# A new order for the first batch of a float32 attention-and-ELU kernel: states and x loaded first on two queues, a weight product in halves, weight sums moved

## The chip, the core and the metric

One core of one Trainium2 chip. The metric is the device time of one execution in microseconds (us). The median of the fast executions counts; ratios are computed as the mean time of one kernel's fast runs over that of the other's in the same rounds, so they are not quite the ratio of the medians quoted. PE is TensorE, PEld its weight loads, DVE VectorE, ACT ScalarE, POOL GpSimd, SP the engine that issues most transfers.

## The reference, cut to what matters

```python
# x: (8, 8, 512, 64), state: (8, 8, 32, 64); w_in: (512, 2048), w_out: (2048, 512); inputs are float64 or float32
scores = scale * x @ state.T          # softmax over the 32 states
xread  = softmax(scores) @ state      # one row per token
scores2 = scale * state @ x.T         # softmax over the 512 tokens
sread  = softmax(scores2) @ x         # one row per state
rows = concat(xread, sread)           # 8 batches of 544 rows of 512
h = rows @ w_in
g = where(h > 0, h, exp(min(h, 0)) - 1)
out = g @ w_out
```

The weights arrive as float64, and the kernel turns each block of 512 columns into float32 itself, with three instructions on ACT (`convert_1`) and four on DVE (`convert_2`).

## The kernel before

For a batch, the kernel multiplies the states of the batch into w_in once ("M", by groups of 512 columns), so that the first product is `attention weights @ M` (F:0 to F:15) and x @ w_in is never formed. ACT takes exp of each block (R), DVE forms the ELU (E, the "max part"), and PE multiplies by w_out. In batch 0 the second product (O:0 to O:15) follows block by block, because w_out is still arriving; from batch 1 on it is a Strassen-like scheme that needs sums of w_out (`weight_sum`).

Batch 0 runs by a written plan. Each word is one step, and each engine keeps the order of its own steps:

```python
plan = """
    w:0.1 w:0.2 kT kTc x:0.0 xc:0.0 w:1.1 x:0.1 xc:0.1 w:1.2 w:2.1 sc:0 mx:0.0 w:3.1 w:2.2
    w:4.1 mx:0.1 tr:0.0 tr:0.1 ae:0.0 tm:0.0 ae:0.1 w:3.2 ps:0.0 w:5.1 tm:0.1 te:0.0 M:0.0
    ...
    tt:1.1 sr:1 O:15 src:1 M:1.0
""".split()
# w:k.1 / w:k.2  conversion of block k on ACT / on DVE
# kT, kTc        transposes of the states on PE, copy on DVE
# x:b.i, xc:b.i  transposes of x on PE, copies on ACT;  sc:b  scores on PE
# mx tr tm su sd tt attention on DVE;  ps pm on POOL;  ae te on ACT
# sT, sTc        transposes of a on PE, copy on ACT;  sr, src  state read on PE, kept by ACT
# M:b.c, Mc:b.c  M for a group of 512 columns on PE, copies;  F R E O  the two products
```

The loads, the sums and the order switch:

```python
def load_states():
    ...
    sync.dma_start(out=raw[m * NS : (m + 1) * NS, :, c], in_=s_v[m, c])   # 8 of them

load_x(0, [scalar])
fetch()                      # one weight block
raw_states = load_states()
for k in range(NRAW - 2):
    fetch()
...
first_batch()
load_x(2, [sync])
for e in (vector, scalar, gpsimd):
    e.on = False             # from here the build's scheduler may reorder these engines
for i in (1, 2, 4, 3):
    weight_sum(i)
for b in range(1, B):
    batch(b)
```

Of the kernel before, what the change touches and what calls it, by code (L numbers as in the profile page):

```python
# [10 lines left out]
FP32 = mybir.dt.float32  # L11
I32 = mybir.dt.int32
U32 = mybir.dt.uint32
# [12 lines left out]
def kernel(  # L26
# [16 lines left out]
    NS = state.shape[2]  # L43
# [37 lines left out]
    def banks(shape, name):  # L81
        return ps_a.tile(shape, FP32, tag="a", name=name)
# [23 lines left out]
        return ap[:, :, None].to_broadcast(list(ap.shape) + [n])  # L106

    ident = cpool.tile([P, P], FP32, name="ident")
    w_in = cpool.tile([P, NP, DF], FP32, name="w_in")
    w_out = cpool.tile([P, FO, DM], FP32, name="w_out")  # L110

    g_all = cpool.tile([P, FO, S], FP32, name="g_all")
# [15 lines left out]
    def load_states():  # L128
        raw = work.tile([P, B, G, D], FP32, tag="w", name="s_sb")
        s_v = state.rearrange("b (m c) n d -> m c n b d", c=G)  # L130
        for m in range(NP):
            for c in range(G):
                sync.dma_start(out=raw[m * NS : (m + 1) * NS, :, c], in_=s_v[m, c])
        return raw

    def turn_states(raw):
# [2 lines left out]
            transpose(ps[:, b], raw[:, b].rearrange("p c d -> p (c d)"))  # L139

    def load_weights(src):
        k = src.shape[-1]
        raw = work.tile([P, 512], moe_w_in.dtype, tag="w", name="raw")
        sync.dma_start(out=raw.rearrange("p (j k) -> p j k", k=k), in_=src)
        return raw

    def low_words(raw):
        return raw.bitcast(U32).rearrange("p (j w) -> p j w", w=2)[:, :, 0]

    def high_words(raw):  # L150
        return raw.bitcast(U32).rearrange("p (j w) -> p j w", w=2)[:, :, 1]

    def convert_1(dst, raw):

# [27 lines left out]
        )  # L182
        vector.tensor_tensor(out=bits, in0=bits, in1=lo, op=ALU.add)

    def load_w_in(c, n):
        cols = slice(c * 512, (c + 1) * 512)
        raw = load_weights(w_in_v[:, n : n + 1, cols])
        return w_in[:, n, cols], raw

    def load_w_out(fo):  # L190
        raw = load_weights(w_out_v[:, fo : fo + 1])
        return w_out[:, fo], raw

    def turn_x(b, i):

# [15 lines left out]
    def by_state(b, name, rhs):  # L211


        ps = banks([P, G, 512], name)
        for m in range(NP):
            for g in range(G):
                d = slice(g * D, (g + 1) * D)
                matmul(
                    ps[m * NS : (m + 1) * NS, g],
                    kT[d, b, m * NS : (m + 1) * NS],  # L220
                    rhs[m][d],
                    start=True,
                    stop=True,
                    tile_position=(g * D, m * NS),
                )
        return ps

    def scores(b):

        st[b, "s_ps"] = by_state(b, "s_ps", [st[b, m] for m in range(NP)])  # L230



# [98 lines left out]
                in_=ps[:, k : k + B // 2].rearrange("p b m s -> p m b s"),  # L332
            )

    def make_m(b, c):

        cols = slice(c * 512, (c + 1) * 512)
        st[b, "m", c] = by_state(b, "m_ps", [w_in[:, m, cols] for m in range(NP)])

    def copy_m(b, c, engines):  # L340
        m_t[b, c] = mpool.tile([P, G, 512], FP32, name="m_sb")
        for g in range(G):
            engines[g](out=m_t[b, c][:, g], in_=st[b, "m", c][:, g])

    def full_m(b, c):
        make_m(b, c)
# [31 lines left out]
    def ffn1_state(fo):  # L378

        ps = ps_h.tile([P, B * NS], FP32, tag="h", name="h_ps")  # L380
        for co in range(NP):
            matmul(
                ps,
                w_in[:, co, fo * P : (fo + 1) * P],
                st["xT"][:, co].rearrange("p b s -> p (b s)"),
                start=(co == 0),
                stop=(co == NP - 1),
            )
        elu(ps, fo)
# [145 lines left out]
    def first_batch():  # L535





        plan = """
            w:0.1 w:0.2 kT kTc x:0.0 xc:0.0 w:1.1 x:0.1 xc:0.1 w:1.2 w:2.1 sc:0 mx:0.0 w:3.1 w:2.2
            w:4.1 mx:0.1 tr:0.0 tr:0.1 ae:0.0 tm:0.0 ae:0.1 w:3.2 ps:0.0 w:5.1 tm:0.1 te:0.0 M:0.0
            w:6.1 w:4.2 ps:0.1 te:0.1 su:0.0 Mc:0.0 su:0.1 pm:0.0 w:8.1 w:6.2 pm:0.1 w:9.1 tt:0.0
            w:7.1 tt:0.1 w:8.2 F:0 w:10.1 F:1 w:7.2 R:0 w:11.1 E:0 w:5.2 F:2 R:1 O:0 R:2 E:1 w:9.2
            w:12.1 E:2 M:0.1 w:10.2 O:1 w:13.1 w:12.2 Mc:0.1 w:14.1 w:13.2 F:3 w:15.1 O:2 w:11.2 R:3
            w:16.1 E:3 w:15.2 F:4 w:17.1 w:16.2 O:3 R:4 w:18.1 E:4 w:14.2 w:19.1 F:5 sd:0.0 w:20.1
            O:4 w:19.2 R:5 w:20.2 w:21.1 F:6 w:22.1 E:5 M:0.2 w:17.2 R:6 F:7 Mc:0.2 w:22.2 w:23.1
            O:5 E:6 w:24.1 w:18.2 R:7 F:8 w:24.2 O:6 R:8 E:7 w:25.1 E:8 w:21.2 w:26.1 F:9 w:25.2 O:7
            w:27.1 w:23.2 R:9 E:9 F:10 sd:0.1 w:27.2 O:8 R:10 E:10 w:28.1 w:26.2 F:11 w:29.1 w:28.2  # L550
            O:9 R:11 w:29.2 w:30.1 w:31.1 M:0.3 E:11 w:30.2 O:10 Mc:0.3 w:31.2 sT:0 F:12 sTc:0 sr:0
            R:12 E:12 O:11 src:0 x:1.0 F:13 xc:1.0 x:1.1 R:13 F:14 xc:1.1 E:13 sc:1 R:14 O:12 mx:1.0
            E:14 mx:1.1 tr:1.0 tr:1.1 ae:1.0 F:15 tm:1.0 ae:1.1 tm:1.1 ps:1.0 sd:1.0 O:13 R:15
            ps:1.1 sd:1.1 te:1.0 E:15 te:1.1 su:1.0 su:1.1 pm:1.0 sT:1 O:14 sTc:1 pm:1.1 tt:1.0
            tt:1.1 sr:1 O:15 src:1 M:1.0
        """.split()
        make_identity(nc, ident)
        o_ps = [o_bank() for c in range(3)]
        o_ps += [ps_h.tile([P, DM], FP32, tag="h", name="o_ps")]
        order = [lambda n=n: load_w_in(0, n) for n in range(NP)]  # L560
        for c in range(1, FC + 1):
            if c < FC:
                order += [lambda c=c, n=n: load_w_in(c, n) for n in range(NP)]
            order += [lambda fo=fo: load_w_out(fo) for fo in range(4 * c - 4, 4 * c)]
        w, h, e = [], {}, {}

        def fetch():
            if len(w) == 28:
                load_x(1, [sync])
            if len(w) < len(order):  # L570
                w.append(order[len(w)]())

        load_x(0, [scalar])
        fetch()
        raw_states = load_states()
        for k in range(NRAW - 2):
            fetch()
        groups = {
            "mx": column_max, "tr": turn_scores, "ae": column_exp, "tm": row_max,
            "ps": row_subtract, "te": row_exp, "su": row_sum, "pm": row_scale,  # L580
            "tt": turn_tokens, "sd": column_total,
        }
        whole = {
            "sc": scores, "sT": turn_state, "sTc": copy_state, "sr": state_read,
            "src": keep_read,
        }
        for step in plan:
            name, _, num = step.partition(":")
            num = [int(i) for i in num.split(".") if i]
            if name == "kT":  # L590
                turn_states(raw_states)
            elif name == "kTc":
                vector.tensor_copy(out=kT, in_=st["k_ps"])
                fetch()
            elif name in groups:
                groups[name](*num)
            elif name in whole:
                whole[name](*num)
            elif name == "w":
                (convert_1, convert_2)[num[1] - 1](*w[num[0]])  # L600
                if num[1] == 2:
                    fetch()
            elif name == "F":
                h[num[0]] = ffn1(0, num[0])
            elif name == "R":
                e[num[0]] = exp_part(h[num[0]])
            elif name == "E":
                max_part(num[0], e[num[0]], h[num[0]])
            elif name == "O":
                ffn2_row(o_ps, num[0])  # L610
            elif name == "x":
                turn_x(*num)
            elif name == "M":
                make_m(*num)
            elif name == "xc":
                copy_x(*num)
            else:
                assert name == "Mc", step
                copy_m(*num, (scalar.copy, scalar.copy))
        copy_m(1, 0, (scalar.copy, vector.tensor_copy))  # L620
        for i in range(2):
            o_sb = opool.tile([P, 2, DM], FP32, name="o_sb")
            for c in range(2):
                (scalar.copy, vector.tensor_copy)[c](out=o_sb[:, c], in_=o_ps[2 * i + c])
            store(0, i, o_sb)

    def batch(b):
        for fo in range(FO):
            elu(ffn1(b, fo), fo)
            if fo % 4 == 1 and fo // 4 + 1 < FC:  # L630
                full_m(b, fo // 4 + 1)
        nxt = b + 1 < B
        hooks = attention(b + 1) if nxt else []
        if b + 2 < B:
# [28 lines left out]
    load_x(2, [sync])  # L663
    for e in (vector, scalar, gpsimd):
        e.on = False
    for i in (1, 2, 4, 3):
        weight_sum(i)
    for b in range(1, B):
        batch(b)
    states()  # L670
# [30 lines left out]
```

## Time and profile before

| | before |
|---|---|
| median of the runs | 797.74 us (797.61 to 797.83) |
| span of the profiled run | 795.6 us |
| PE / DVE / ACT busy | 95% / 43% / 40% |
| F:0, first product of batch 0, starts | 43.27 us |
| O:0, second product of batch 0, starts | 51.44 us |
| batch 1's first product, second half of its first block | 143.32 us |

The shares of the whole span hide the point: DVE and ACT are near full in the first 110 us and half idle afterwards, and PE is the reverse. The stretch up to O:0 and the seam between batch 0 and batch 1 are the two places where PE is not full.

### The profile page before, as it was taken

Reading aid. Unit: us, or ns where it says so; the run is one execution under the profiler, and the core shown is the slowest. Engines: PE = TensorE matmul, PEld = TensorE weight load, DVE = VectorE, ACT = ScalarE, POOL = GpSimd, SP = SyncE. Lnnn points to the kernel's source line nnn. Section 1 sums busy time; section 2 is a strip of 40 time slices with the busy share of each in tenths; the row PEclk is TensorE's granted clock in tenths of the full one; section 3 lists DMA queues with packets and bytes.
Section 4 is the critical chain, followed back from the end, with each engine's and each line's share of the span. In section 5 each row is a group of like instructions: output and inputs, shape, how many; then the busy total and the mean of one; then the engine's idle time right before and its main releaser. Section 6 shows DMA issues by size and latency. Waiting matters only on the chain.

```text
span 795.6 us, 9330 instructions
## 1 busy us (share of the span) xinstructions
PE 756.3 (95%) x3808; PEld 500.9 (63%) x3808; DVE 343.4 (43%) x577; ACT 320.7 (40%) x596; POOL 34.1 (4%) x38
## 2 busy tenths in 40 slices
PE   2389999999999999999999999999999999999996
PEld 1034454358863887368845885488647884588885
DVE  1899958546024721464135612472146313511140
ACT  2889853562136311642055213631264206400420
POOL 0100002002000010002000200010000200000000
PEclk9979999999999999999999999999999999999999
DMA  9757200400300030001100030003000000000001
GB/s 220 276 158 222 103 1 1 106 1 1 80 27 0 2 80 27 1 0 45 37 26 1 1 80 27 0 1 80 27 0 1 29 0 27 1 26 1 28 0 27
DMA packets 42795, 35.21 MB, mean 44 GB/s; under 512 B 36352, under 2 KB 36352, under 8 KB 42752
## 3 DMA queue, kind: packets, MB, share of 16 engines
q1 hardware_dynamic: 38592, 33.56, 14.6%
q10 hardware_dynamic: 4160, 1.05, 0.7%
q8 instruction: 30, 0.49, 0.3%
q14 instruction: 13, 0.11, 0.0%
HBM read 25.69 MB, written 8.91 MB: 43 GB/s over the span
## 4 chain that ended last, share of the span: by engine, by line
PE 93%; DVE 4%; DMA 1%; ACT 0%; issue 0%; ACTq 0%
PE o_ps L92 52%; PE h_ps L92 32%; PE m_ps L92 4%; PE xT_ps L92 2%; DVE w_in L92 1%; PE s_ps L92 1%; DMA x_sb<-in_x_dram 1%; DVE t_w L92 1%; PE sr_ps L92 1%; PE sT_ps L92 1%; DVE total_t L92 1%; DMA s_sb<-in_state_dram 0%; DVE w_out L92 0%; ACT xT L92 0%; PE k_ps L92 0%; DVE aT L92 0%
## 5 line engine op out<-in xcount | busy, mean ns | idle before, releaser
L92 PE MATMUL o_ps<-w_out,g_all 128*128 128x256 f32 (+1 forms) x1088 | 274.8, 406 | 0.0
L92 PEld LDWEIGHTS o_ps<-w_out,g_all 128*128 128x128 f32 x1088 | 204.2, 190 | 62.8 <-issue 35.8
L92 PE MATMUL h_ps<-aT,m_sb 128*128 128x512 f32 x512 | 232.1, 603 | 9.4 <-DVE aT L92 7.9
L92 PEld LDWEIGHTS h_ps<-aT,m_sb 128*128 128x128 f32 x512 | 96.1, 192 | 139.5 <-issue 112.2
L92 DVE SCALAR_TENSOR_TENSOR g_all<-e_sb,h_ps 128x512 f32<-128x512 f32 (+1 forms) x144 | 94.5, 657 | 193.8 <-ACT e_sb L92 193.8
L92 ACT ACTIVATE e_sb<-h_ps 128x512 f32<-128x512 f32 (+1 forms) x144 | 82.4, 572 | 96.3 <-PE h_ps L92 96.2
L92 ACT COPY o_sb<-o_ps 128x256 f32<-128x256 f32 (+1 forms) x62 | 23.3, 378 | 240.2 <-PE o_ps L92 240.2
L92 PE MATMUL o_ps<-t_w,s 128*128 128x256 f32 x480 | 109.1, 380 | 0.0
L92 PEld LDWEIGHTS o_ps<-t_w,s 128*128 128x128 f32 x480 | 90.2, 190 | 16.8 <-ACT o_sb L92 5.0
L92 ACT ACTIVATE e_sb<-e_sb 128x512 f32<-128x512 f32 (+1 forms) x144 | 87.2, 606 | 4.5
L92 DVE TENSOR_TENSOR o_sb<-o_sb,o_ps 128x256 f32<-128x256 f32 x45 | 18.6, 414 | 158.1 <-issue 82.8
L92 PE MATMUL o_ps<-t_w,g_all 128*128 128x256 f32 x240 | 54.2, 379 | 0.0
L92 PEld LDWEIGHTS o_ps<-t_w,g_all 128*128 128x128 f32 x240 | 45.6, 190 | 6.2
L92 PE MATMUL m_ps<-w_in,kT 64*32 64x512 f32 x512 | 37.6, 615 | 6.9 <-ACT a_s L92 6.9
L92 ACT ACTIVATE raw<-raw 128x512 f32<-128x512 uint32 x64 | 43.6, 681 | 1.0
L92 POOL TENSOR_TENSOR t_sb<-t_sb,top_t 128x512 f32<-128x512 f32 x16 | 16.9, 1061 | 573.0 <-DVE top_t L92 560.3
L92 DVE COPY m_sb<-m_ps 128x512 f32<-128x512 f32 x28 | 19.2, 685 | 42.0 <-ACT m_sb L92 42.0
L92 ACT COPY xT<-xT_ps 128x512 f32<-128x512 f32 x32 | 17.2, 589 | 35.0 <-PE xT_ps L92 35.0
L92 PE MATMUL h_ps<-xT_state,w_in 128*128 128x256 f32 x128 | 27.8, 379 | 0.0
L92 PEld LDWEIGHTS h_ps<-xT_state,w_in 128*128 128x128 f32 x128 | 24.3, 190 | 3.3
L92 PEld LDWEIGHTS m_ps<-w_in,kT 64*32 64x32 f32 x512 | 6.0, 105 | 31.3 <-issue 20.9
L92 ACT COPY m_sb<-m_ps 128x512 f32<-128x512 f32 x36 | 20.3, 576 | 8.5 <-PE m_ps L92 8.5
(54 smaller groups left out, 388.2 us busy)
## 6 DMA issues: line engine op xcount, KB each, us to landing
raw<-in_moe_w_in_dram SPq DMA_DIRECT2D x16, 512.0 KB, 5.0
raw<-in_moe_w_out_dram SPq DMA_DIRECT2D x16, 512.0 KB, 4.9
out_dram<-o_sb SPq DMA_DIRECT2D x16, 512.0 KB, 2.7
x_sb<-in_x_dram SPq DMA_DIRECT2D x28, 256.0 KB, 4.9
x_sb<-in_x_dram ACTq DMA_DIRECT2D x4, 256.0 KB, 6.9
s_sb<-in_state_dram SPq DMA_DIRECT2D x8, 64.0 KB, 5.1
out_dram<-o_sb SPq DMA_DIRECT2D x8, 64.0 KB, 1.7
```

What stands on the lines that cost most here:

```text
L92: ins = getattr(self.engine, name)(*args, **kw)
```

## The change

The intent was to let PE start sooner. States and x are loaded before any weight, half on each of two queues. w_in is loaded and stored by half groups of 256 columns with all four row blocks (two of them per load), so that M's first half needs two converted blocks instead of four. The plan has a new order on all engines. The sums of w_out are written inside batch 1's first product.

```diff
-    w_in = cpool.tile([P, NP, DF], FP32, name="w_in")
+    w_in = cpool.tile([P, 2 * FC, NP, 256], FP32, name="w_in")
...
-                sync.dma_start(out=raw[m * NS : (m + 1) * NS, :, c], in_=s_v[m, c])
+                (sync, scalar)[c].dma_start(out=raw[m * NS : (m + 1) * NS, :, c], in_=s_v[m, c])
...
+    def load_w_in(c, k):
+        h, n = divmod(k, 2)
+        rows = slice(2 * n, 2 * n + 2)
+        cols = slice(c * 512 + h * 256, c * 512 + (h + 1) * 256)
+        return w_in[:, 2 * c + h, rows], load_weights(w_in_v[:, rows, cols])
...
-            w:0.1 w:0.2 kT kTc x:0.0 xc:0.0 w:1.1 x:0.1 xc:0.1 w:1.2 w:2.1 sc:0 mx:0.0 w:3.1 w:2.2
+            kT kTc x:0.0 xc:0.0 w:0.1 x:0.1 xc:0.1 w:0.2 w:1.1 sc:0 mx:0.1 w:2.1 tr:0.1 tr:0.0
+            tm:0.1 w:3.1 tm:0.0 ps:0.1 mx:0.0 w:1.2 ps:0.0 ae:0.1 ae:0.0 te:0.1 sT:0 sd:0.0 sd:0.1
+            te:0.0 su:0.1 sTc:0 su:0.0 pm:0.1 w:4.1 M:0.0.0 w:3.2 pm:0.0 Mc:0.0.0 w:7.1 sr:0 tt:0.1
... (the rest of the plan is new as well)
-        load_x(0, [scalar])
-        fetch()
         raw_states = load_states()
-        for k in range(NRAW - 2):
+        load_x(0, [sync, scalar])
+        for k in range(NRAW - 1):
             fetch()
...
             if fo % 4 == 1 and fo // 4 + 1 < FC:
                 full_m(b, fo // 4 + 1)
+            if b == 1 and fo % 4 == 3:
+                weight_sum((1, 2, 4, 3)[fo // 4])
...
-    for i in (1, 2, 4, 3):
-        weight_sum(i)
```

More of the change, by code (lines that the diff above doesn't have):

```diff
@@ L141, in load_weights @@
     def load_weights(src):
-        k = src.shape[-1]
-        raw = work.tile([P, 512], moe_w_in.dtype, tag="w", name="raw")
-        sync.dma_start(out=raw.rearrange("p (j k) -> p j k", k=k), in_=src)
+        _, n, k = src.shape
+        raw = work.tile([P, n, k], moe_w_in.dtype, tag="w", name="raw")
+        sync.dma_start(out=raw, in_=src)
         return raw
     def low_words(raw):
-        return raw.bitcast(U32).rearrange("p (j w) -> p j w", w=2)[:, :, 0]
+        return raw.bitcast(U32).rearrange("p n (j w) -> p n j w", w=2)[:, :, :, 0]
     def high_words(raw):
-        return raw.bitcast(U32).rearrange("p (j w) -> p j w", w=2)[:, :, 1]
+        return raw.bitcast(U32).rearrange("p n (j w) -> p n j w", w=2)[:, :, :, 1]
     def convert_1(dst, raw):
@@ L183, in convert_2 @@
         vector.tensor_tensor(out=bits, in0=bits, in1=lo, op=ALU.add)
-    def load_w_in(c, n):
-        cols = slice(c * 512, (c + 1) * 512)
-        raw = load_weights(w_in_v[:, n : n + 1, cols])
-        return w_in[:, n, cols], raw
+    def load_w_in(c, k):
[3 more added lines that the diff above has]
+        return w_in[:, 2 * c + h, rows], load_weights(w_in_v[:, rows, cols])
     def load_w_out(fo):
         raw = load_weights(w_out_v[:, fo : fo + 1])
-        return w_out[:, fo], raw
+        return w_out[:, fo : fo + 1], raw
     def turn_x(b, i):
@@ L214, in by_state @@
         ps = banks([P, G, 512], name)
+        _, j, n = rhs[0].shape
         for m in range(NP):
@@ L218, in by_state @@
                 matmul(
-                    ps[m * NS : (m + 1) * NS, g],
+                    ps[m * NS : (m + 1) * NS, g, : j * n].rearrange("p (j n) -> p j n", j=j),
                     kT[d, b, m * NS : (m + 1) * NS],
@@ L228, in scores @@
     def scores(b):
-        st[b, "s_ps"] = by_state(b, "s_ps", [st[b, m] for m in range(NP)])
+        st[b, "s_ps"] = by_state(b, "s_ps", [st[b, m][:, None] for m in range(NP)])
     def column_max(b, g):
@@ L333, in turn_read, with make_m @@
             )
-    def make_m(b, c):
-        cols = slice(c * 512, (c + 1) * 512)
-        st[b, "m", c] = by_state(b, "m_ps", [w_in[:, m, cols] for m in range(NP)])
+    def make_m(b, c, h=None):
+        halves = slice(2 * c, 2 * c + 2) if h is None else slice(2 * c + h, 2 * c + h + 1)
+        st[b, "m", c] = by_state(b, "m_ps", [w_in[:, halves, m] for m in range(NP)])
     def copy_m(b, c, engines):
@@ L343, in copy_m, with copy_half @@
             engines[g](out=m_t[b, c][:, g], in_=st[b, "m", c][:, g])
+    def copy_half(b, c, h):
+        if h == 0:
+            m_t[b, c] = mpool.tile([P, G, 512], FP32, name="m_sb")
+        scalar.copy(
+            out=m_t[b, c][:, :, h * 256 : (h + 1) * 256], in_=st[b, "m", c][:, :, :256]
+        )
     def full_m(b, c):
@@ L383, in ffn1_state @@
                 ps,
-                w_in[:, co, fo * P : (fo + 1) * P],
+                w_in[:, fo // 2, co, fo % 2 * P : (fo % 2 + 1) * P],
                 st["xT"][:, co].rearrange("p b s -> p (b s)"),
@@ L541, in first_batch @@
         plan = """
-            w:0.1 w:0.2 kT kTc x:0.0 xc:0.0 w:1.1 x:0.1 xc:0.1 w:1.2 w:2.1 sc:0 mx:0.0 w:3.1 w:2.2
-            w:4.1 mx:0.1 tr:0.0 tr:0.1 ae:0.0 tm:0.0 ae:0.1 w:3.2 ps:0.0 w:5.1 tm:0.1 te:0.0 M:0.0
-            w:6.1 w:4.2 ps:0.1 te:0.1 su:0.0 Mc:0.0 su:0.1 pm:0.0 w:8.1 w:6.2 pm:0.1 w:9.1 tt:0.0
-            w:7.1 tt:0.1 w:8.2 F:0 w:10.1 F:1 w:7.2 R:0 w:11.1 E:0 w:5.2 F:2 R:1 O:0 R:2 E:1 w:9.2
-            w:12.1 E:2 M:0.1 w:10.2 O:1 w:13.1 w:12.2 Mc:0.1 w:14.1 w:13.2 F:3 w:15.1 O:2 w:11.2 R:3
@@ L547, in first_batch @@
-            w:16.1 E:3 w:15.2 F:4 w:17.1 w:16.2 O:3 R:4 w:18.1 E:4 w:14.2 w:19.1 F:5 sd:0.0 w:20.1
-            O:4 w:19.2 R:5 w:20.2 w:21.1 F:6 w:22.1 E:5 M:0.2 w:17.2 R:6 F:7 Mc:0.2 w:22.2 w:23.1
-            O:5 E:6 w:24.1 w:18.2 R:7 F:8 w:24.2 O:6 R:8 E:7 w:25.1 E:8 w:21.2 w:26.1 F:9 w:25.2 O:7
-            w:27.1 w:23.2 R:9 E:9 F:10 sd:0.1 w:27.2 O:8 R:10 E:10 w:28.1 w:26.2 F:11 w:29.1 w:28.2
-            O:9 R:11 w:29.2 w:30.1 w:31.1 M:0.3 E:11 w:30.2 O:10 Mc:0.3 w:31.2 sT:0 F:12 sTc:0 sr:0
@@ L552, in first_batch @@
-            R:12 E:12 O:11 src:0 x:1.0 F:13 xc:1.0 x:1.1 R:13 F:14 xc:1.1 E:13 sc:1 R:14 O:12 mx:1.0
-            E:14 mx:1.1 tr:1.0 tr:1.1 ae:1.0 F:15 tm:1.0 ae:1.1 tm:1.1 ps:1.0 sd:1.0 O:13 R:15
-            ps:1.1 sd:1.1 te:1.0 E:15 te:1.1 su:1.0 su:1.1 pm:1.0 sT:1 O:14 sTc:1 pm:1.1 tt:1.0
-            tt:1.1 sr:1 O:15 src:1 M:1.0
+            kT kTc x:0.0 xc:0.0 w:0.1 x:0.1 xc:0.1 w:0.2 w:1.1 sc:0 mx:0.1 w:2.1 tr:0.1 tr:0.0
+            tm:0.1 w:3.1 tm:0.0 ps:0.1 mx:0.0 w:1.2 ps:0.0 ae:0.1 ae:0.0 te:0.1 sT:0 sd:0.0 sd:0.1
@@ new lines, in first_batch @@
+            te:0.0 su:0.1 sTc:0 su:0.0 pm:0.1 w:4.1 M:0.0.0 w:3.2 pm:0.0 Mc:0.0.0 w:7.1 sr:0 tt:0.1
+            tt:0.0 w:4.2 F:0 src:0 w:8.1 w:2.2 F:1 R:0 w:5.1 E:0 M:0.0.1 w:8.2 Mc:0.0.1 R:1 F:2
+            w:5.2 w:9.1 O:0 E:1 w:10.1 w:9.2 R:2 F:3 w:10.2 w:6.1 M:0.1.0 O:1 E:2 Mc:0.1.0 w:6.2 R:3
+            w:12.1 E:3 F:4 w:7.2 w:11.1 O:2 w:12.2 w:13.1 R:4 w:11.2 M:0.1.1 F:5 w:14.1 w:13.2 O:3
+            R:5 Mc:0.1.1 E:4 w:16.1 E:5 w:14.2 F:6 w:17.1 M:0.2.0 w:16.2 F:7 R:6 w:15.1 E:6 O:4
+            w:17.2 Mc:0.2.0 w:18.1 w:15.2 F:8 R:7 w:18.2 O:5 w:21.1 E:7 R:8 w:21.2 M:0.2.1 w:19.1
@@ new lines, in first_batch @@
+            O:6 E:8 w:23.1 w:19.2 Mc:0.2.1 F:9 w:23.2 w:24.1 O:7 w:25.1 w:24.2 w:20.1 w:25.2 F:10
+            R:9 O:8 w:20.2 w:22.1 E:9 R:10 w:22.2 M:0.3.0 w:26.1 F:11 E:10 O:9 Mc:0.3.0 w:26.2 R:11
+            w:27.1 E:11 M:0.3.1 w:29.1 w:27.2 F:12 O:10 R:12 w:29.2 Mc:0.3.1 w:30.1 E:12 F:13 w:31.1
+            w:30.2 O:11 R:13 w:31.2 w:28.1 E:13 x:1.0 w:28.2 F:14 xc:1.0 x:1.1 R:14 F:15 xc:1.1 E:14
+            sc:1 R:15 O:12 mx:1.0 mx:1.1 ae:1.0 tr:1.0 ae:1.1 tr:1.1 tm:1.0 sT:1 tm:1.1 ps:1.0 O:13
@@ L556, in first_batch @@
+            sd:1.0 sTc:1 sd:1.1 E:15 ps:1.1 te:1.0 su:1.0 te:1.1 pm:1.0 su:1.1 sr:1 pm:1.1 tt:1.0
+            O:14 src:1 tt:1.1 M:1.0 O:15 Mc:1.0
         """.split()
@@ L559, in first_batch @@
         o_ps += [ps_h.tile([P, DM], FP32, tag="h", name="o_ps")]
-        order = [lambda n=n: load_w_in(0, n) for n in range(NP)]
+        order = [lambda k=k: load_w_in(0, k) for k in range(4)]
         for c in range(1, FC + 1):
             if c < FC:
-                order += [lambda c=c, n=n: load_w_in(c, n) for n in range(NP)]
+                order += [lambda c=c, k=k: load_w_in(c, k) for k in range(4)]
             order += [lambda fo=fo: load_w_out(fo) for fo in range(4 * c - 4, 4 * c)]
@@ L567, in fetch @@
         def fetch():
-            if len(w) == 28:
-                load_x(1, [sync])
             if len(w) < len(order):
                 w.append(order[len(w)]())
-        load_x(0, [scalar])
-        fetch()
+            elif 1 not in x_t:
+                load_x(1, [sync])
         raw_states = load_states()
-        for k in range(NRAW - 2):
+        load_x(0, [sync, scalar])
+        for k in range(NRAW - 1):
             fetch()
@@ L618, in first_batch @@
                 assert name == "Mc", step
-                copy_m(*num, (scalar.copy, scalar.copy))
-        copy_m(1, 0, (scalar.copy, vector.tensor_copy))
+                if len(num) == 3:
+                    copy_half(*num)
+                else:
+                    copy_m(*num, (scalar.copy, scalar.copy))
         for i in range(2):
```

## The prediction

> **What bounds the kernel now.** I read the busy slices first, then the chain of waits in order of time up to 220 us, then windows of the first 60 us, then the timeline at both ends of batch 0.
>
> The 40 slices of the page:
>
> ```profile
> PE   2389999999999999999999999999999999999996
> ...
> DVE  1899958546024721464135612472146313511140
> ACT  2889853562136311642055213631264206400420
> ...
> DMA  9757200400300030001100030003000000000001
> ```
>
> TensorE (PE) is full from about 43 us to the end. A slice is 19.9 us, so only the first two slices and the seam between batches are open to this change. In those slices VectorE (DVE) and ScalarE (ACT) are full too: they turn 32 blocks of float64 weights into float32. The chain of waits in order of time:
>
> ```profile
> 12.77 0.35 issue
> 13.12 1.95 PE k_ps L92 x8
> ...
> 16.37 1.98 PE xT_ps L92 x8
> ...
> 22.64 2.07 PE s_ps L92 x16
> ...
> 43.27 8.17 PE h_ps L92 x12
> 51.44 3.43 PE o_ps L92 x8
> ...
> 134.75 5.65 DVE t_w L92 x5
> 140.39 2.27 DVE w_out L92 x2
> 142.66 0.61 DVE m_sb L92
> 143.32 2.84 PE h_ps L92 x6
> ```
>
> Columns: start, length, what. The states arrive at 12.77, the scores end at 24.7, the first product of batch 0 (F:0, "h_ps") starts at 43.27, its second product (O:0, "o_ps") at 51.44, batch 1 at about 142. Between 24.7 and 43.27 the chain runs in DVE, which does attention and six conversions by turns.
>
> The chain puts 9.6 us of w_out sums (t_w 1.70 + 5.65, w_out 2.27) on the path before batch 1. That overstates them. The timeline of PE there:
>
> ```profile
> 139.57 1.09 PE L92 MATMUL m_ps<-w_in,kT 64*32 64x512 f32 x16
> 141.41 1.12 PE L92 MATMUL h_ps<-aT,m_sb 128*128 128x512 f32 x2 [0.75 <-ACT m_sb L92]
> 143.32 2.84 PE L92 MATMUL h_ps<-aT,m_sb 128*128 128x512 f32 x6 [0.79 <-DVE m_sb L92]
> ```
>
> While DVE did the sums, PE still had O:14, O:15 and M of batch 1 to do. PE idles only 0.75 and 0.79 us (brackets). Counting instruction starts, M ends at 140.6, the second half of batch 1's first product starts at 143.32 and one half costs 0.86, so the equivalent gapless start is 143.32 - 0.86 = 142.46. The seam can give at most about 142.46 - 140.6 = 1.9 us, not 9.6.
>
> **What the Trainium skill says.** "TensorE: Matmul & The Clock Gate", Part 1, What's actually happening: an idle array runs at half clock, and needs about 3.4 us of sustained work to get the full one. The trace agrees in the two-microsecond windows (columns: length; busy us and count of PE, PEld, DVE, ACT, POOL; granted clock; DMA share; GB/s):
>
> ```profile
> 42.00:44.00 2.00, 0.73 (x1) 0.50 (x2) 2.00 (x4) 1.97 (x4) 0.00 (x0) 0.50 0.29 70
> 44.00:46.00 2.00, 2.00 (x4) 0.71 (x3) 1.90 (x5) 0.33 (x1) 0.00 (x0) 0.50 0.48 193
> ...
> 48.00:50.00 2.00, 2.00 (x5) 0.73 (x5) 1.74 (x5) 1.97 (x4) 0.00 (x0) 0.78 0.69 215
> ```
>
> The clock is 0.50 to about 48.9, 5.6 us after F:0 began, so three F take 8.17 us where 12 x 0.43 = 5.16 is the later rate. The new order meets the same cold start. "DMA: Bandwidth & Descriptors", Issuing engines are not separate DMA queues: transfers issued by several engines share the same 16 engines, so a second queue saves issue time only. The trace agrees in part: from 6 to 10 us, with both queues in use, the windows show 203 to 213 GB/s, against 387 in 20 to 30 us when only 4 KB rows move. "SBUF — State Buffer", Who interferes with whom: some VectorE modes and GpSimd lock each other out. The trace agrees: next to a GpSimd instruction a pair of DVE TENSOR_SCALAR took 1.60 us instead of 0.88, three times before F:0. The new order keeps those four GpSimd instructions, so I keep that loss.
>
> **The change, part by part.**
>
> *Loads.* Before, x is on ACT's queue while SP's carries one weight block and then the states, which end at 12.77. After, states then x come first, halves on each queue. States are 0.52 MB and x 1.05 MB, all in 256-byte rows. At 205 GB/s that is 2.6 and 5.1 us, and the first bytes move at 1.8 in the trace before. So I expect states at 5 to 6 us and x at about 10.3 (9.5 plus the completion). k_ps (1.95) and its copy (1.24) then lie before x, off the path: done by about 9. The x transposes start near 10.5 instead of 16.37. From there to the end of the scores the order is unchanged in kind (transposes, copy, one conversion on ACT, transposes, copy, scores), 8.33 us before (16.37 to 24.70). The first weight block lands near 12.5 and may delay that by a few tenths. Scores end: 19.0, 5.7 earlier.
>
> *DVE from scores to F:0.* One conversion is 2.25 us (four starts in the timeline, 100.59 to 102.84). Before, 24.73 to F:0 held four conversions on DVE after w:1 (2.2, 3.2, 4.2, 6.2: 9.0) and attention (two column maxima at 0.76, four transposes at 0.63, two row maxima at 0.62, two sums at 1.07: 7.4), 16.4, plus about 2.2 of GpSimd loss: 18.6, as observed (18.5). After: two conversions (1.2 and 3.2: 4.5), the same attention and the two column totals (0.6): 12.5. I add 1.7 for GpSimd: 14.2. F:0 at 33.2, 10.1 earlier.
>
> *F:0 to O:0.* PE cold again: F:0 and F:1 until about 39.5. Then M's second half (about 0.6), its ACT copy (0.6 and two handoffs), F:2 at 1.72. O:0 near 42.7, against 51.44: 8.7 earlier. The halves of M are what permits F:0 after two weight blocks; the second half puts its copy between F:1 and F:2, which costs about 1 us.
>
> *PE from O:0 to batch 1.* Before: 140.6 - 51.44 = 89.2. By durations: 16 O at 3.43, 13 F at 1.72, four M at 1.02, four transposes groups at 0.87, two state reads and one scores at about 1.03 come to 87.9; the rest is that a product after such a tiled group takes 3.63 in the chain instead of 3.43. After: batch 0's transposes of a and its state read have gone before F:0 (-1.9), and six M halves at about 0.6 + 0.2 replace three M at 1.22 (+1.1). 88.4. So batch 1 starts near 42.7 + 88.4 = 131.1, without the 1.9 of the seam, since M of batch 1 now precedes O:15 and both its copies go to ACT. Gain: 142.46 - 131.1 = 11.4.
>
> *Is DVE fast enough for this?* From the scores to the last conversion, its queue holds before 31 conversions less one (67.5), 12 max parts at 0.64 (7.7) and attention (8.0) = 83.2; the trace has 24.73 to 110.27, 85.5. After, two more max parts and one more conversion: 86.8 + 2.3 = 89.1, ending at 108. PE then needs O:12 not before 42.7 + 88.4 - 16.6 = 114.5 (16.6 = four O, transposes, state read, M). It is in time with about 6 us to spare at the end, less in the middle. ACT's sum over the same stretch is 86.6 by like counting, also just enough. I allow 0.7 us for stalls between three queues that are all over 90% full.
>
> *w_out sums in batch 1.* Eight TENSOR_TENSOR of 1024 columns, 1.15 us each: 9.2 us, a pair after every fourth F. Four F take 6.9 us plus M 1.0; DVE then holds four max parts (2.8) and one copy (0.7), so 2.3 more fits. With three h banks, a max part may come 1.3 us late (two F at 1.72 less 2.1 for the two activations and the max part); a pair makes it late by about that much. I allow 0.4 us. PE is otherwise unchanged; so are conversions, whose blocks remain 512 columns.
>
> Sum: -11.4 + 0.7 + 0.4 = -10.3, about 787.4. Against that, the loads may come a microsecond or two sooner than I take, and PE may be warm at F:0, because a's transposes, M and the state read now run just before it (worth up to 2.8). I move the middle to 786.0.
>
> **Rivals.** (1) *The whole DVE gain arrives*: F:0 near 32 with a warm PE, no stall: O:0 at 39, batch 1 at 127.5, 782 to 783. For it: the chain before F:0 is purely DVE. Against it: the idle array just before. (2) *Conversions become the bound*: the new order has done six blocks at O:0 where the old one had done eight or nine, so PE may wait inside batch 0 and give back 3 to 5 us: 789 to 791. For it: DVE and ACT at 96% before. Against: the sums above. (3) *Weights arrive late*: they are now behind 1.57 MB of small rows on the same queue, in 2 KB runs. If conversions start at 17 instead of 13, F:0 slides by 2 to 4 us: 789. (4) *The sums were the bound and vanish*: -9.6 more, 777. The PE timeline speaks against it.
>
> **Range and chances.** The terms carry about 1.5 us each for the loads, the cold start and the stalls: 781.5 to 790.5. Faster by over 2% needs below 781.8, rival 1 complete and more: 0.13. Slower by 2% would need 16 us lost where little work is added: 0.01.
>
> **What would show it.** Right: x transposes at 10 to 11 us, scores ending near 19, F:0 at 32 to 34, O:0 at 41 to 44, batch 1 at 129 to 133, PE without gaps over 1 us in batch 1's first product. Wrong: PE idle before o_ps on w_out or w_in in batch 0 (rival 2), ACT idle before its first conversion beyond 15 us (rival 3), clock at 1.00 from F:0 (rival 1).

## The result

The changed kernel took 787.49 us (786.91 to 787.80, four runs) against 797.78 us in the same rounds: ratio 0.9871, interval 0.9853 to 0.9888. That is 1.3% faster, inside the predicted range and inside "within 2%". The profiled span went from 795.6 to 785.6.

The busy slices of the page after the change (a slice is now 19.6 us):

```profile
PE   4599999999999999999999999999999999999996
...
DVE  2999969464135602472045512471146213611230
ACT  4799873642056213631165204621263206400420
...
DMA  9566400301200030003000020003000000000001
```

PE's first slices rise from 2, 3, 8 to 4, 5, 9. DVE begins its full stretch in the second slice in both kernels and ends it in the sixth. The chain of waits after, in order of time (start, length, what):

```profile
11.07 1.34 PE xT_ps L92 x5
...
16.70 2.07 PE s_ps L92 x16
...
33.09 3.54 PE h_ps L92 x4
...
40.29 1.98 PE h_ps L92 x4
42.28 3.43 PE o_ps L92 x8
...
119.29 1.62 DVE t_w L92
...
130.88 1.70 DVE w_out L92
132.58 0.63 DVE aT L92
...
133.34 2.81 PE h_ps L92 x6
```

The scores end at 18.77 (16.70 + 2.07) instead of 24.7. F:0 starts at 33.09 instead of 43.27, and O:0 at 42.28 instead of 51.44. The second half of batch 1's first block starts at 133.34 instead of 143.32. The sums of w_out ("t_w", and "w_out" for the sum made in place) still run at 119 to 133 us, before batch 1, although the text has them inside batch 1's first product.

Counted as the prediction did, batch 1 starts without a gap at 133.34 - 0.86 = 132.48 instead of 142.46, 9.98 us earlier. What follows is 653.1 us long in both kernels (795.6 - 142.46 and 785.6 - 132.48). So the whole gain is made before batch 1, and nothing of it is given back later.

PE's own waits from O:0 to batch 1 are two, in brackets in its timeline:

```profile
118.13 1.09 PE L92 MATMUL sT_ps<-ident,a_s 128*128 128x128 f32 x8 [1.19 <-DVE t_sb L92]
...
133.34 2.81 PE L92 MATMUL h_ps<-aT,m_sb 128*128 128x512 f32 x6 [0.52 <-DVE aT L92]
```

The first is new: the transposes of a wait until DVE and ACT have taken turns on the scores of batch 1. The second replaces the two waits of 0.75 and 0.79 at the seam before; now the last transpose of batch 1's attention weights is late, behind a sum on DVE.

| step | predicted | measured |
|---|---|---|
| x transposes start | 10.5 | 9.18 for the first, 11.07 for the last five |
| scores end | 19.0 | 18.77 |
| F:0 | 33.2 | 33.09 |
| O:0 | 42.7 | 42.28 |
| O:0 to batch 1 on PE, with 0.7 of stalls | 89.1 | 90.2 (132.48 - 42.28) |
| added in batch 1's first product | 0.4 | 0 |
| sum of the terms | 787.4 | 787.49 |
| middle | 786.0 | 787.49 |

### The profile page after: what moved, and what is told of

Read it like the earlier page. It is cut to its first block, busy times and chain, and to the rows that moved or that the text cites. A ratio compares the mean times of both kernels' runs of the same rounds, so it can differ in the third digit from the quotient of the medians.

```text
span 785.6 us, 9457 instructions
## 1 busy us (share of the span) xinstructions
PE 756.6 (96%) x3872; PEld 502.2 (64%) x3872; DVE 342.8 (44%) x576; ACT 321.5 (41%) x597; POOL 34.9 (4%) x38
## 4 chain that ended last, share of the span: by engine, by line
PE 93%; DVE 4%; DMA 1%; ACT 1%; issue 0%; ACTq 0%
PE o_ps L92 52%; PE h_ps L92 32%; PE m_ps L92 4%; PE xT_ps L92 2%; PE s_ps L92 1%; DVE t_w L92 1%; DMA x_sb<-in_x_dram 1%; PE sr_ps L92 1%; DVE w_in L92 1%; PE sT_ps L92 1%; DVE total_t L92 1%; DVE top L92 0%; DMA s_sb<-in_state_dram 0%; DVE t_sb L92 0%; DVE aT L92 0%; DVE top_t L92 0%
## 5 line engine op out<-in xcount | busy, mean ns | idle before, releaser
L92 PEld LDWEIGHTS o_ps<-t_w,s 128*128 128x128 f32 x480 | 90.2, 190 | 16.7 <-ACT o_sb L92 5.0
L92 PE MATMUL m_ps<-w_in,kT 64*32 64x512 f32 (+1 forms) x576 | 36.2, 561 | 1.2 <-ACT aT_s L92 1.2
```

The costliest lines, as they stand in the source:

```text
L92: ins = getattr(self.engine, name)(*args, **kw)
```

## The experiments

Four questions stood after the result. Did the loads or the new order give the gain, or only both? Are the sums worth anything where they stand? Were conversions close to being the bound? Was the cold array before F:0 still to be had? Eleven runs, in three groups; each group was timed beside the kernel before on the same chip (medians 797.54 to 797.65). For one and the same built order the fast executions reach from 786.6 to 787.8, and x2 and z3, one kernel in two groups, have fast medians of 786.14 and 787.36; so a difference below about 1.2 us between two runs is not resolved. Part of the scatter is the landing of x, which ends between about 10.1 and 11.2 us in the profiled executions with the new loads. Where I quote smaller ones, they are from the traces, which fix the place but are one execution each.

### x1: the sums written before batch 1 again

```diff
-            if b == 1 and fo % 4 == 3:
-                weight_sum((1, 2, 4, 3)[fo // 4])
...
+    for i in (1, 2, 4, 3):
+        weight_sum(i)
     for b in range(1, B):
```

> The changed kernel with the w_out sums written before batch 1 again, as the kernel before had them. Theory: where the sums stand in the text makes no difference, because the scheduler of the build places them by readiness in the last part of batch 0 in either case; 787.5 us within 0.4. Rival: writing them inside batch 1's first product is worth part of the 1.9 us that the seam lost before; then this run takes 788.5 to 789.5.

Measured 786.82 us (786.60 to 787.79), ratio 0.9864. This is 0.7 below the changed kernel's median, a little outside my number, and not slower as the rival asks. The built program settles it: on PE, DVE and ACT the instructions stand in the same order as in the changed kernel. The order in which the two traces record them agrees. So this part of the change did nothing. DVE is free to be reordered from batch 1 on, and the scheduler fetched the sums forward into the end of batch 0 from either place in the text. The two medians differ by scatter alone, and I use 786.8 as the reference for the runs on the same chip.

### x2 and z3: the sums really inside batch 1's first product

```diff
     def batch(b):
+        vector.on = b == 1
         for fo in range(FO):
...
+        vector.on = False
         nxt = b + 1 < B
```

> The changed kernel, with VectorE held to the order of the text during batch 1's first product, so that each pair of sums really comes after every fourth max part. Theory: VectorE loses 9.2 us of work before the last transpose of attention weights of batch 1, PE no longer waits 0.5 us there, and the sums hide under the matmuls of batch 1's first product: 786.7 to 787.2, with batch 1's first product still 30.5 us. Rival: a pair of sums makes max parts late, PE waits for h banks by about 0.4 us at each of three places: 788 to 788.5.

> The run with the sums held in batch 1's first product again, for a profile at full clock: the first had one execution of 1343 us at half clock among three of 786.1 to 786.5. Expected: 786.0 to 786.6, PE's wait of 0.5 us before batch 1 gone, batch 1's first product as long as in the changed kernel. If the execution at half clock belongs to this kernel, it comes again in some of these; if it belongs to the chip, it does not.

x2's fast executions took 786.10 to 786.45, a little under the expected 786.7 to 787.2. One execution, the profiled one, took 1343.33 us, with a mean clock of 0.567; its time is used for nothing. z3 repeats the kernel: 787.36 us (786.30 to 788.09), ratio 0.9870, and no execution at half clock in four. z3's median is above its expected 786.0 to 786.6. So neither number came out, one on each side, and the expected half microsecond is not resolved. z3 ran on another chip, so it does not say either whether the half clock belongs to the kernel or to the chip. The place is: PE's and DVE's timelines of z3 have

```profile
131.46 3.60 PE L92 MATMUL h_ps<-aT,m_sb 128*128 128x512 f32 x8
...
162.64 3.62 PE L92 MATMUL o_ps<-w_out,g_all 128*128 128x256 f32 x16
```

```profile
124.47 0.71 DVE L92 STREAM_TRANSPOSE aT<-t_sb 128x512 f32<-128x512 f32 x1 [0.65 <-POOL t_sb L92]
...
141.64 2.35 DVE L92 TENSOR_TENSOR t_w<-w_out 128x1024 f32<-128x1024 f32 x2
```

The last transpose of batch 1's weights is done at 125 instead of 133, PE runs into batch 1 with no bracket, and the sums stand in batch 1's first product. That product lasts 31.2 us there (131.46 to 162.64) and 31.2 in the changed kernel (132.48 to 163.68 in the same view). The 0.4 us that I had allowed for late max parts does not occur: a pair of sums fits.

### x3 and x4: the order alone, the loads alone

x3 is the changed kernel with the old loads; x4 is the kernel before with the new loads.

```diff
# x3, on the changed kernel; the states go back to the one queue too
-        raw_states = load_states()
-        load_x(0, [sync, scalar])
-        for k in range(NRAW - 1):
+        load_x(0, [scalar])
+        fetch()
+        raw_states = load_states()
+        for k in range(NRAW - 2):
# x4, on the kernel before: the reverse, and in its plan
-            w:0.1 w:0.2 kT kTc x:0.0 xc:0.0 w:1.1 x:0.1 xc:0.1 w:1.2 w:2.1
+            kT kTc x:0.0 xc:0.0 w:0.1 x:0.1 xc:0.1 w:0.2 w:1.1 w:1.2 w:2.1
```

> The changed kernel with the loads of the kernel before: one weight block first, then the states on the one queue, x on the other; the order of the engines stays new. Theory: states arrive at 12.8 again, scores end near 24.7 instead of 18.8, and since PE is full from its second product on, all 5.9 us go to the end: 793.0 to 793.8. Rival: conversions on VectorE and ScalarE set the pace, and the early weight block lets them begin at 8 instead of 13; then no more than 3 us is lost, 790.5 or less.

> The kernel before with the new loads alone; the first weight block is converted between the two copies of x, so that the scores do not wait for it, and the rest of the order is the old one. Theory: scores end near 18.8 to 19, but two conversions instead of one then lie on VectorE ahead of the first column maximum, so F:0 starts near 39 and the gain is about 4 us: 793.0 to 794.5. With the first expectation it says how much the loads give alone, and how much only together with the order. Rival: conversions set the pace, their sum on VectorE is unchanged and now starts later, so nothing is gained: 797 or more.

| | old order | new order |
|---|---|---|
| old loads | 797.54 | 792.83 (x3) |
| new loads | 792.93 (x4) | 786.82 (x1) |

The chains of waits of x3 and then of x4, at F:0 and O:0:

```profile
38.39 3.79 PE h_ps L92 x4
...
47.82 3.43 PE o_ps L92 x8
```

```profile
38.44 8.36 PE h_ps L92 x12
46.80 3.43 PE o_ps L92 x8
```

Each alone gives 4.6 to 4.7 us, both give 10.7. They are two separate shortenings of the same chain. The old loads cost the new order 6.0 us (792.83 - 786.82), as much as the scores come later (24.05 against 18.77 in the two chains, 5.3) within the scatter. The new loads give the old order less than that, because w:0.2 and w:1.2 then both stand on DVE ahead of the first column maximum; F:0 was expected near 39 there and came at 38.44. Both rivals, that conversions set the pace of batch 0, fall: x3 lost more than 3 us, and x4 gained. These runs do not separate the second queue from the new sequence of the loads, nor, inside the new order, the halves of M from the new sequence on DVE.

### y1: a warm array for F:0

```diff
+        idle = ps_h.tile([P, 512], FP32, tag="h", name="idle")
...
             elif name in whole:
                 whole[name](*num)
+                for k in range({"sc": 3, "sT": 1, "sr": 1}.get(name, 0) if num[0] == 0 else 0):
+                    matmul(idle, ident, warm, start=True, stop=True)   # a bank nobody reads
```

> The changed kernel with five matmuls of no use on PE, three after the scores and one each after the transposes of a and after the state read of batch 0, into a bank that nobody reads. Theory: F:0 starts at 33.1 with a cold array and costs 3.54 us instead of 1.72; the activations of F:0, the copy of M's second half and F:2 follow it, so a warm array brings O:0 from 42.3 to 40.5 and the whole gain reaches the end, because conversions have slack: 784.8 to 785.4. Rival (conversions are the bound): O:0 comes earlier but PE then waits on converted weights in batch 0 and less than 0.5 us is gained, 786.4 or more.

Measured 786.60 us (786.16 to 787.71), ratio 0.9865: not resolved from 786.82, and inside the rival's 786.4 or more, not my 784.8 to 785.4. PE's timeline of the changed kernel, then of y1:

```profile
33.09 5.25 PE L92 MATMUL h_ps<-aT,m_sb 128*128 128x512 f32 x8 [1.47 <-DVE aT L92]
38.27 0.66 PE L92 MATMUL m_ps<-w_in,kT 64*32 64x256 f32 x16
```

```profile
32.96 3.70 PE L92 MATMUL h_ps<-aT,m_sb 128*128 128x512 f32 x8 [0.51 <-DVE aT L92]
37.54 0.67 PE L92 MATMUL m_ps<-w_in,kT 64*32 64x256 f32 x16 [0.88 <-DVE w_in L92]
```

F:0 and F:1 together fall from 5.25 to 3.70 us, so the array is warm. But M's second half then waits 0.88 us for a conversion on DVE. O:0 comes at 40.92, 1.4 earlier than in the changed kernel, but the second half of batch 1's first block at 132.49, only 0.85 earlier. The rest is lost after O:0. From there to the scores of batch 1 PE takes 70.59 us (40.76 to 111.35) against 70.10 in the changed kernel (42.12 to 112.22), because O:3 and O:4 start late. Their weight loads wait for conversions on DVE (timeline of y1):

```profile
57.88 0.30 PEld L92 LDWEIGHTS o_ps<-w_out,g_all 128*128 128x128 f32 x2 [0.76 <-DVE w_out L92]
...
65.83 0.30 PEld L92 LDWEIGHTS o_ps<-w_out,g_all 128*128 128x128 f32 x2 [0.85 <-DVE w_out L92]
```

So the rival is right, in its number and in its cause: with F:0 warm, conversions hold PE once before O:0 and twice after it.

### y2 and z1: the wait of 1.19 us before batch 1

```diff
# y2: the transposes of a one product later
-            ... tm:1.0 sT:1 tm:1.1 ps:1.0 O:13
+            ... tm:1.0 tm:1.1 ps:1.0 O:13 sT:1
# z1: the x transposes of batch 1 one product earlier
-            w:30.2 O:11 R:13 w:31.2 w:28.1 E:13 x:1.0 w:28.2 F:14 xc:1.0 x:1.1 R:14 F:15 xc:1.1 E:14
-            sc:1 R:15 O:12
+            w:30.2 x:1.0 xc:1.0 O:11 R:13 x:1.1 w:31.2 w:28.1 xc:1.1 E:13 w:28.2 F:14 sc:1 R:14 F:15
+            E:14 R:15 O:12
```

> The changed kernel with the transposes of a of batch 1 after O:13 on PE instead of before it. Theory: PE's wait of 1.2 us for VectorE's and ScalarE's turns on the scores is the part of the step from O:0 to batch 1 that the prediction left out; O:13 fills it, and 785.6 to 786.0 results. Rival: VectorE's chain of batch 1's attention, not PE, decides when batch 1 starts, the wait moves to the last transpose, and the time stays at 786.6 to 787.2.

> The changed kernel with batch 1's two groups of x transposes one product earlier on PE, so that F:15 and O:12 both lie between the scores and the transposes of a. In the last trial the wait of 1.2 us only moved to the state read, since that then followed without a product between. Theory: now every turn has a product under it, PE waits nowhere from O:0 to O:15, and 1.2 us less than the 786.8 of the same built order results, 785.4 to 785.9; the wait of 0.5 us on the last transpose of batch 1's weights stays or grows, as VectorE has its sums there. Rival: that last transpose takes up the whole gain and the time stays at 786.5 to 787.

y2 took 787.08 us (786.48 to 787.40) and z1 787.24 us (786.43 to 787.55). Neither gained; both numbers are near the rivals' (786.6 to 787.2 and 786.5 to 787). PE's timeline of y2 and then of z1:

```profile
122.03 1.10 PE L92 MATMUL sr_ps<-x_sb,aT_s 128*32 128x64 f32 x64 [1.16 <-ACT aT_s L92]
```

```profile
117.31 1.07 PE L92 MATMUL sT_ps<-ident,a_s 128*128 128x128 f32 x8 [0.99 <-DVE t_sb L92]
```

In y2 the wait moved to the state read, which then had no product between it and the copy that it needs. In z1 PE had more work between scores and transposes, yet the wait stayed: DVE began on the scores about 1 us after they were there, because the max part of F:14 came first in its order, and the two transposes then waited 1.34 and 0.84 us for ACT's exponentials. My theory for y2 is wrong as written, and so is its rival: the wait moved, but not to the last transpose. My theory for z1, that PE would wait nowhere from O:0 to O:15, is wrong too. What the wait would be worth if it were truly filled stays open; no run here removed it.

### y3, y4 and z2: matmuls of no use from the start, and all together

y3 adds matmuls of no use to the changed kernel from 1.36 us on: ten before the states arrive, six after their transposes, three after each group of x transposes, five wide ones after the scores, and one wide one after each of the transposes of a, M's first half and the state read. y4 is y3 with x2's held sums and y2's order. z2 is y4 with z1's order in place of y2's.

```diff
+        idle = ps_h.tile([P, 512], FP32, tag="h", name="idle")
+        small_ones = {"kT": 6, "x:0.0": 3, "x:0.1": 3}
+        wide_ones = {"sc:0": 5, "sT:0": 1, "M:0.0.0": 1, "sr:0": 1}
+        for k in range(10):
+            matmul(idle[:, :P], ident, ident, start=True, stop=True)
         for step in plan:
+            ...  # after each step its number of idle matmuls
```

> The changed kernel with matmuls of no use in every idle stretch of PE from 1.3 us on. Theory: transposes and scores before F:0 also run at full rate, the scores end near 16.9 instead of 18.8, limited by the first conversion on ScalarE between the two copies of x, and F:0 is warm: 3.5 us in all against the changed kernel, 783.0 to 784.0. Rivals: the first weight block has not landed by 12.7, then 784 to 785; or conversions become the bound of batch 0, with PE waiting on w_out, 785 or more.

> The warm array of the run before this, with the sums really in batch 1's first product and the transposes after O:13. If the three effects add (3.5, 0.5 and 1.2): 781.5 to 782.5. If VectorE's attention chain decides batch 1's start, then about 783. Its profile also shows whether sums in batch 1's first product make PE wait: the theory says that product stays at 30.5 us, the rival of late max parts 31.5 or more.

> The best of the runs so far (warm array, sums held in batch 1's first product) with the new place of the x transposes instead of the later transposes of a. Theory: VectorE has no sums ahead of its last transpose, so nothing takes the 1.2 us back: 782.6 to 783.2 against 784.2. Rival: VectorE's attention chain after its last conversion is the bound there, 784 again.

y3 took 785.00 us (784.16 to 785.14), ratio 0.9840; y4 784.17 us (783.29 to 784.60), ratio 0.9830; z2 784.22 us (783.24 to 784.89) on another chip, ratio 0.9828. All three are faster than the changed kernel, by 1.8 to 2.6 us against 786.8, but less than the sums of my terms, and outside the ranges of my theories. In y3 the second group of x transposes takes 1.09 us instead of 1.97, the scores start at 16.02, but DVE's first column maximum starts only at 17.37, since the conversion w:0.2 occupies DVE until then. Hence O:0 at 39.56 instead of 42.28, of which 2.2 us are left at batch 1 (131.13 against 133.34). F:0 and F:1 are warm there (3.70 us), and as in y1 M's second half waits 0.88 us, and O:3 and O:4 lose 0.5 us to conversions (70.61 us from O:0 to batch 1's scores, 39.39 to 110.00). That is y3's second rival, 785 or more with PE waiting on w_out. z2 came out at its rival's 784; whether for the rival's reason is not tested.

y4 was to answer whether conversions bound batch 0, and does not. Its PE timeline at F:0:

```profile
30.76 5.40 PE L92 MATMUL h_ps<-aT,m_sb 128*128 128x512 f32 x8 [1.96 <-DVE aT L92]
```

F:0 and F:1 take 5.40 us in y4, and also in z2: the array was cold again, after the same matmuls of no use as in y3 and nearly the same wait before F:0 (1.96 and 1.93 us; 1.95 in y3). Why it was warm in one of these executions and cold in two is not shown. y4's O:0 comes at 39.84, 2.4 us earlier than in the changed kernel, because DVE too was earlier: its first column maximum starts at 16.54 instead of 18.79. So PE came no nearer to the conversions, and it takes 70.1 us from O:0 to the scores of batch 1 in both (39.68 to 109.78, and 42.12 to 112.22, in the timelines). The slack of the conversions is read from y1 and y3 instead. There the time from the first column maximum to O:0 fell from 23.49 to 22.27 and 22.19 us, and PE lost 0.5 us after O:0. My estimate from these numbers is 0.7 to 0.8 us of slack after O:0.

## Why the prediction was right or wrong, point by point

**What bounds.** Right. PE is full from O:0 on, so O:0's shift is nearly the gain: 9.2 us of shift, 10.0 of gain.

**The seam is worth 1.9 us, not 9.6.** Right, and the step that mattered most against an easy misreading. The chain of waits had 9.6 us of sums on it before, and 10.3 after, while the bracketed waits of PE were 1.54 before. z3, with the sums truly gone from the seam, loses only the wait of 0.52 us. x1 does not bear on this, since its built order is that of the changed kernel. The 1.9 us were not won, though: waits of 1.19 and 0.52 us stand in their place.

**Loads, scores, F:0, O:0.** Right within half a microsecond each. Two errors cancelled, which is luck: x landed at 11.03 instead of 10.3, and three of the eight first transposes were done while the last rows of x were still on the way, which saved 0.6 us. x3 and x4 show that loads and order each carry about half.

**O:0 to batch 1.** Here the step "PE from O:0 to batch 1" was short by 1.8 us (88.4 predicted, 90.2 measured), of which the separate allowance of 0.7 covered a part. It priced PE's work correctly (an M half is 0.59 in the chain, and a product after it takes 3.63 against 3.43) but had no wait in it, since "M of batch 1 now precedes O:15" seemed to fill the seam. The mis-sized term is the 1.19 us before the transposes of a and the 0.52 us before batch 1. The allowance was for stalls between busy queues inside batch 0; the trace of the changed kernel shows none there after O:0.

**Is DVE fast enough.** Right for this change, but by less than the 6 us at the end suggest; the prediction only says "less in the middle". In the changed kernel the conversion for O:4 ends at 66.44 and O:4 starts at 66.80, and y1 and y3, with PE 1.2 to 1.3 us nearer, wait there.

**The sums in batch 1's first product.** Wrong in its premise: the sums are not there. I read the place in the text as the place in time, with the line that frees VectorE's order in the same text. The allowance of 0.4 us was not needed even with the sums held there (z3, y4).

**The middle.** The sum of the terms was 787.4, and the measured time is 787.49; that they agree within 0.1 is partly luck, since the waits that were left out and the allowances that were not needed offset each other. I then moved it to 786.0 for earlier loads and a possibly warm array. Neither came: x was, if anything, later, and F:0 took 3.54 us, its matmuls 0.85 us apart against 0.43 later, the cold rate. That last adjustment, of 1.4 us, is the step that failed. (A slip of reading did no harm: between 24.7 and 43.27 the chain has four conversions, as the prediction's own sum counts, and not six.)

**The rivals.** The first (everything arrives, 782 to 783) did not come by itself; with a warm array forced it reached 785.0. The second (conversions bind) did not come in the changed kernel: PE waits on no weight from O:0 on, and x3 and x4 speak against it. It is close by, though: once F:0 is warm (y1, y3) conversions take 0.88 us just after F:1 and 0.5 us at O:3 and O:4. The third (weights late) did not happen: ACT began its first conversion at 13.40, directly after its copy of x. The fourth was excluded by z3.

## What to carry to other kernels

Where one engine is full, read its own bracketed waits at a seam and not the length of the chain that passes through another engine; here the chain said 9.6 us and the waits 1.54. Moving an instruction in the text of a kernel whose build reorders that engine may move nothing, so compare the built orders before pricing it. At the cold start of this kernel, loads and order shortened the same chain and added up (10.7 us together, 4.6 and 4.7 alone). Matmuls of no use warmed F:0 in the profiled executions of y1 and y3 but not of y4 and z2, so look at each trace; and with F:0 warm, part of the gain went to the engine next in line, which had under 1 us to spare.

## What the Trainium skill lacked or had wrong

- "TensorE: Matmul & The Clock Gate", Part 1, has the half rate of an idle array and about 3.4 us of sustained work to warm it. The half rate agrees (F:0's matmuls 0.85 us apart, 0.43 later); in the kernel before, the half clock lasted 5.6 us after F:0 began. The page warns that recorded clock events are not to be fully trusted, and here is a case: the granted clock reads full while the matmuls run at the cold rate. In the changed kernel the windows from 20 to 40 us give 1.00, and F:0 lies in them. Windows of the changed kernel (length; busy us and count of PE, PEld, DVE, ACT, POOL; clock; DMA share; GB/s):

```profile
33.00:36.00 3.00, 2.91 (x4) 1.36 (x5) 2.86 (x7) 1.02 (x2) 0.00 (x0) 1.00 0.94 332
```

- The same page explains half clock by idle time. In x2 one execution took 1343.33 us, with PE full and a clock of 0.56 in the windows from 60 us on; the other seven executions of that kernel were at full clock. No run here shows the cause:

```profile
core 0: 1341.5 us, clock 0.567
```

- "TensorEngine Tiling (Array Packing)", Key Properties, says that a change of tiling mode drains TensorE, and gives no time for it. Here the first product after a tiled group (M, scores) takes 3.63 us in the chain instead of 3.43, so about 0.2 us per group, in and out together; with M in halves there are more of them. That this is the drain is not shown.
- No page has what a scheduler may do to the place of an instruction; x1 shows that a changed place in the text left the built order as it was.
